# Exponentials as the stationary operand of the value product, 128-row output tiles over two batches, and a hand-written TensorE order

## The chip, the cores and the metric

The kernel runs on one core of one Trainium2 chip. The metric is the time of one execution on the device in microseconds (us), as the device reports it; medians of several executions are given. Every execution was classed as fast or slow (slow when over 1.5% above the fastest of its kernel). In the profiles PE is TensorE (the matrix engine), DVE is VectorE, ACT is ScalarE and POOL is GpSimd. TensorE writes its results to PSUM tiles; that DVE or ACT copies a tile out, so that it can be used again, is called its eviction.

## The reference, cut to what matters

```python
# attention: q, k, v are (8 batches, 12 heads, 448 rows, 64), fp32
q_n = q / (np.linalg.norm(q, axis=-1, keepdims=True) + 1e-06)
k_n = k / (np.linalg.norm(k, axis=-1, keepdims=True) + 1e-06)
attn = softmax(q_n @ k_n.T / tau)                # per head, 448 x 448, tau = 0.1
x = concat_heads(attn @ v)                       # (8, 448, 768)
# token mixing (T = 256), then channel mixing (C = 1536)
h  = np.maximum(x.T @ w_tok1, 0.0) @ w_tok2
u  = x + h.T
h2 = np.maximum(u @ w_ch1, 0.0) @ w_ch2
out = u + h2                                     # (8, 448, 768) fp32
```

## The kernel before

Rows are handled in four chunks of 112. Heads are handled in pairs, six pairs per batch, 48 pairs in all; a half of a batch is three pairs and is loaded together. The mixer of one batch is spread over the slots of the next batch's pairs. The parts that the change and the argument touch:

```python
SC, NCH, NPAIR = 112, 4, 6

def emit_attention_prep(b, pj, qkv_tiles):       # one pair: normalise q and k
    # ... cut: qt, kt are the pair's part of the loaded half
    sq16 = att.tile([SC, 2, 2, NCH, E], FP16, ...)
    nc.gpsimd.tensor_mul(out=sq16[:, 0], in0=qt[:], in1=qt[:])
    nc.gpsimd.tensor_mul(out=sq16[:, 1], in0=kt[:], in1=kt[:])
    nc.vector.tensor_reduce(out=ssq[:], in_=sq16[:], axis=AXX.X, op=ALU.add)
    nc.scalar.activation(out=lssq[:], in_=ssq[:], func=AF.Ln)
    nc.scalar.activation(out=rnorm[:], in_=lssq[:], func=AF.Exp, scale=-0.5)
    # ... cut: four tensor_tensor on gpsimd give qn and kn

def emit_attention_pv(b, pj):                    # v stationary, exp(scores) moving
    for hh in range(2):
        psO = ps.tile([E2, S], FP32, ...)        # 66 x 448, transposed output
        for i, c in enumerate(reversed(range(NCH))):
            nc.tensor.matmul(psO[:], vt[:, hh, c, :], pt16[:, c // 2, hh, c % 2, :],
                             start=(i == 0), stop=(i == NCH - 1))
        # ... cut: copied to SBUF as fp32 (ot), ACT for hh == 0, DVE for hh == 1

def emit_attention_bridge(b, pj, x16):           # transposed back, divided by the sum
    for hh in range(2):
        for c in range(NCH):
            nc.tensor.transpose(psT[:, c, :], ot[:, c * SC:(c + 1) * SC], id32[:E2, :E2])
        nc.vector.reciprocal(out=rec[:], in_=psT[:, :, E])
        nc.vector.tensor_tensor(out=x16[...], in0=psT[:, :, 0:E], in1=_bcast_free(rec[:], E),
                                op=ALU.mult)

# mixer slice 5: second channel product, 112-row tiles of one batch
for c in range(NCH):
    for dh in range(NDH):
        for ct_i in range(CT):                   # 12 matmuls
            nc.tensor.matmul(psF[:], gt16[:, ct_i, c * SC:(c + 1) * SC], wc2t[...], ...)
        for tt_i in range(TT):                   # 2 more: the token product, recomputed
            nc.tensor.matmul(psF[:], w2t[:, tt_i, c * SC:(c + 1) * SC], rt16[...], ...)
        nc.vector.tensor_tensor(out=ostage[...], in0=psF[:], in1=x16[...], op=ALU.add)

# main loop: everything is left to the scheduler; weights are loaded as fp32 and cast on DVE
for sl in range(NSLOT):
    # ... cut: load, prep(sl), tpose(sl-2), score(sl-3), pv(sl-4), bridge(sl-5), a mixer slice
```

Of the kernel before, what the change touches and what calls it, by code (L numbers as in the profile page):

```python
# [11 lines left out]
AXX = mybir.AxisListType  # L13

# [9 lines left out]
def kernel(  # L24
# [26 lines left out]
    E2 = E + 2  # L51
    inv_tau = 1.0 / float(tau)
    EPS_NORM = 1e-6

    cst = ctx.enter_context(tc.tile_pool(name="cst", bufs=1))
    wpool = ctx.enter_context(tc.tile_pool(name="wpool", bufs=1))
    stage = ctx.enter_context(tc.tile_pool(name="stage", bufs=3))
    qkv = ctx.enter_context(tc.tile_pool(name="qkv", bufs=3))
    att = ctx.enter_context(tc.tile_pool(name="att", bufs=4))
    ath = ctx.enter_context(tc.tile_pool(name="ath", bufs=4))  # L60
    ptp = ctx.enter_context(tc.tile_pool(name="ptp", bufs=4))
    xp = ctx.enter_context(tc.tile_pool(name="xp", bufs=2))
    mix = ctx.enter_context(tc.tile_pool(name="mix", bufs=1))
# [3 lines left out]
    psm = ps  # L67
# [9 lines left out]
    id32 = cst.tile([128, 128], FP32, name="id32")  # L77
    nc.gpsimd.memset(id32[:], 0.0)
    nc.gpsimd.affine_select(out=id32[:], in_=id32[:], compare_op=ALU.not_equal,
                            fill=1.0, base=0, pattern=[[-1, 128]], channel_multiplier=1)  # L80

    w1t = wpool.tile([SC, NCH, T], FP16, name="w1t")
    w2t = wpool.tile([128, TT, S], FP16, name="w2t")
    wc1t = wpool.tile([128, DT, C], FP16, name="wc1t")
    wc2t = wpool.tile([128, CT, D], FP16, name="wc2t")

    _weight_jobs = []

    def _staged_weight(dst_tile_ap, dram_ap, shape, nm, nchunks):
        def job():  # L90
            st = stage.tile(list(shape), FP32, name=f"ws_{nm}", tag="wst")
            nc.sync.dma_start(out=st[:], in_=dram_ap)
            last = shape[-1]
            cw = (last + nchunks - 1) // nchunks
            for ci in range(nchunks):
                lo, hi = ci * cw, min(last, (ci + 1) * cw)
                nc.vector.tensor_copy(out=dst_tile_ap[..., lo:hi], in_=st[..., lo:hi])  # L97
        return job

    _weight_jobs.append(_staged_weight(w1t[:], moe_w_tok1.rearrange("(c p) t -> p c t", p=SC),  # L100
                                       (SC, NCH, T), "w1", 1))
    _weight_jobs.append(_staged_weight(w2t[:], moe_w_tok2.rearrange("(tt p) s -> p tt s", p=128),
                                       (128, TT, S), "w2", 1))
    for dt_i in range(DT):
        _weight_jobs.append(_staged_weight(wc1t[:, dt_i, :], moe_w_ch1[dt_i * 128:(dt_i + 1) * 128, :],
                                           (128, C), f"wc1_{dt_i}", 3))
    for ct_i in range(CT):
        _weight_jobs.append(_staged_weight(wc2t[:, ct_i, :], moe_w_ch2[ct_i * 128:(ct_i + 1) * 128, :],
                                           (128, D), f"wc2_{ct_i}", 2))

    def emit_weight_loads():
        while _weight_jobs:
            _weight_jobs.pop(0)()

    def emit_qkv_half(b, half):
        h0 = 6 * half
        tiles = {}
        for nm, src in (("q", q), ("k", k)):
            t = qkv.tile([SC, 6, NCH, E], FP32, name=f"{nm}h_{b}_{half}", tag=f"{nm}h")
            nc.sync.dma_start(out=t[:].rearrange("p g c e -> p (g c) e"),  # L120
                              in_=src[b, h0:h0 + 6].rearrange("g (c p) e -> p (g c) e", p=SC))
            tiles[nm] = t
        vt = qkv.tile([SC, 6, NCH, E2], FP16, name=f"vh_{b}_{half}", tag="vh")
        nc.gpsimd.dma_start(out=vt[:, :, :, 0:E].rearrange("p g c e -> p (g c) e"),
                            in_=v[b, h0:h0 + 6].rearrange("g (c p) e -> p (g c) e", p=SC))
        nc.gpsimd.memset(vt[:, :, :, E:E + 2].rearrange("p g c e -> p (g c) e"), 0.0)
        nc.gpsimd.memset(vt[:, :, :, E:E + 1].rearrange("p g c e -> p (g c) e"), 1.0)
        tiles["v"] = vt
        return tiles

    pipe = {}

    def emit_attention_prep(b, pj, qkv_tiles):
        poff = 2 * (pj % 3)
        qt = qkv_tiles["q"][:, poff:poff + 2]
        kt = qkv_tiles["k"][:, poff:poff + 2]
        vt = qkv_tiles["v"][:, poff:poff + 2]

        sq16 = att.tile([SC, 2, 2, NCH, E], FP16, name=f"sq16_{b}_{pj}", tag="sq16")
        nc.gpsimd.tensor_mul(out=sq16[:, 0], in0=qt[:], in1=qt[:])  # L140
        nc.gpsimd.tensor_mul(out=sq16[:, 1], in0=kt[:], in1=kt[:])  # L141
        ssq = att.tile([SC, 2, 2, NCH], FP32, name=f"ssq_{b}_{pj}", tag="ssq")
        nc.vector.tensor_reduce(out=ssq[:], in_=sq16[:], axis=AXX.X, op=ALU.add)  # L143
        lssq = att.tile([SC, 2, 2, NCH], FP32, name=f"lssq_{b}_{pj}", tag="lssq")
        nc.scalar.activation(out=lssq[:], in_=ssq[:], func=AF.Ln)  # L145
        rnorm = att.tile([SC, 2, 2, NCH], FP32, name=f"rnorm_{b}_{pj}", tag="rnorm")
        nc.scalar.activation(out=rnorm[:], in_=lssq[:], func=AF.Exp, scale=-0.5)  # L147

        qn = att.tile([SC, NCH, 2, E], FP16, name=f"qn_{b}_{pj}", tag="qn")
        kn = att.tile([SC, NCH, 2, E], FP16, name=f"kn_{b}_{pj}", tag="kn")  # L150
        for g in range(2):
            nc.gpsimd.tensor_tensor(out=qn[:, :, g, :], in0=qt[:, g],  # L152
                                    in1=_bcast_free(rnorm[:, 0, g], E), op=ALU.mult)
            nc.gpsimd.tensor_tensor(out=kn[:, :, g, :], in0=kt[:, g],  # L154
                                    in1=_bcast_free(rnorm[:, 1, g], E), op=ALU.mult)
        pipe[(b, pj)] = {"qn": qn, "kn": kn, "vt": vt, "h0": 2 * pj}

    def emit_attention_tpose(b, pj):
        st = pipe[(b, pj)]
        qT = att.tile([128, S], FP16, name=f"qT_{b}_{pj}", tag="qT")  # L160
        kT = att.tile([128, S], FP16, name=f"kT_{b}_{pj}", tag="kT")
        for src, dst, tg in ((st["qn"], qT, "q"), (st["kn"], kT, "k")):
            pst = ps.tile([128, NCH, SC], FP16, name=f"pst{tg}_{b}_{pj}", tag="b")
            for c in range(NCH):
                nc.tensor.transpose(pst[:, c, :], src[:, c], id16[:SC, :SC])  # L165
            nc.vector.tensor_copy(out=dst[:], in_=pst[:])
        st["qT"], st["kT"] = qT, kT

    def emit_attention_score(b, pj):
        st = pipe[(b, pj)]  # L170
        qT, kT, h0 = st["qT"], st["kT"], st["h0"]
        pt16 = ptp.tile([SC, 2, 2, 2, S], FP16, name=f"pt16_{b}_{pj}", tag="pt16")
        for cg in range(2):
            psS = ps2.tile([SC, 2, 2, 512], FP32, name=f"psS_{b}_{pj}_{cg}", tag="b2")
            for j in range(2):
                c = 2 * cg + j
                for hh in range(2):
                    hb = hh * 64
                    nc.tensor.matmul(psS[:, hh, j, 0:S],  # L179
                                     kT[hb:hb + 64, c * SC:(c + 1) * SC],  # L180
                                     qT[hb:hb + 64, :],
                                     start=True, stop=True)
            nc.scalar.activation(out=pt16[:, cg], in_=psS[:, :, :, 0:S],  # L183
                                 func=AF.Exp, scale=inv_tau)
        st["pt16"] = pt16

    def emit_attention_pv(b, pj):
        st = pipe[(b, pj)]
        pt16, vt, h0 = st["pt16"], st["vt"], st["h0"]
        st["ot"] = {}  # L190
        for hh in range(2):
            hid = h0 + hh
            psO = ps.tile([E2, S], FP32, name=f"psO_{b}_{hid}", tag="b")
            for i, c in enumerate(reversed(range(NCH))):
                nc.tensor.matmul(psO[:], vt[:, hh, c, :], pt16[:, c // 2, hh, c % 2, :],
                                 start=(i == 0), stop=(i == NCH - 1))
            ot = ath.tile([E2, S], FP32, name=f"ot_{b}_{hid}", tag="ot")
            if hh == 0:
                nc.scalar.copy(out=ot[:], in_=psO[:])
            else:  # L200
                nc.vector.tensor_copy(out=ot[:], in_=psO[:])
            st["ot"][hh] = ot

    def emit_attention_bridge(b, pj, x16):
        st = pipe.pop((b, pj))
        h0 = st["h0"]
        for hh in range(2):
# [145 lines left out]
```

## Time and profile before

| | before |
|---|---|
| median of 3 runs | 622.88 us (619.04 to 623.16) |
| span of the profiled execution | 622.3 us |
| PE (TensorE matmul) busy | 523.1 us, 84% |
| DVE / ACT / POOL busy | 265.2 / 245.5 / 246.2 us |
| first TensorE matmul | 21.9 us |
| warm TensorE work, from the timeline | 466 us |

The last row is an estimate: for each kind of matmul the median distance from one start to the next, times the count (for the scores, which start in fours, about 0.5 us for four). It is what TensorE would need if it were never idle and always at full clock.

From the page of the kernel before: the busy line, two rows of the span in 40 slices (busy tenths of PE, granted TensorE clock in tenths) and the chain of work that ended last.

```profile
PE 523.1 (84%) x3424; PEld 330.4 (53%) x3424; DVE 265.2 (43%) x572; ACT 245.5 (39%) x337; POOL 246.2 (40%) x344
...
PE   0365888998878988789778897888989999999997
...
PEclk9978899799898988989988899888998999999999
...
PE 63%; POOL 19%; ACT 8%; DVE 3%; issue 3%; DMA 2%; SPq 0%; POOLq 0%; DVEq 0%; ACTq 0%
```

No engine but PE is near its limit, and PE itself has an 8 or a 7 in most slices. The timeline of the kernel before shows the pattern. Columns: start, duration, engine, line, operation, what is written and read; in brackets the idle time before it and what ended it.

```profile
300.54 1.65 ACT L183 ACTIVATE pt_4_1_3049<-psS_1_0_3050 112x1792 f16<-112x1792 f32 x1
...
302.24 0.58 PE L179 MATMUL psS_1_1_3056<-qT_1_2819,kT_1_2820 64*112 64x448 f16 x4 [1.81 <-ACT pt_4_1_3049 L183]
...
309.24 1.65 ACT L183 ACTIVATE pt_4_2_3148<-psS_2_0_3149 112x1792 f16<-112x1792 f32 x1
...
310.93 0.59 PE L179 MATMUL psS_2_1_3155<-qT_2_3035,kT_2_3036 64*112 64x448 f16 x4 [1.80 <-ACT pt_4_2_3148 L183]
```

Once per pair the second score group waits 1.8 us for the exponential that frees the only score buffer. The waits view of TensorE lists 61.3 us of waits for ACT in 36 places.

### The profile page before, as it was taken

What the parts mean: (1) busy time and instruction counts of PE and PEld (TensorE: products, weight loads), DVE (VectorE), ACT (ScalarE), POOL (GpSimd) and SP (SyncE); (2) the same over time, 40 slices, a digit from 0 to 9 for tenths busy, and PEclk for the clock granted to TensorE, in tenths of its full rate; (3) what the DMA queues carried; (4) which work ended last, traced back from release to release, by engine and by line L of the source; (5) the groups of instructions that cost most, each with busy time, mean ns of one, the idle gap of its engine ahead of it and who ended that gap; (6) DMA issues with size and microseconds to landing.
All of it is one profiled execution on the core that took longest, in us unless ns stands there. A gap on an engine that the chain in (4) does not pass through costs nothing.

```text
span 622.3 us, 8520 instructions
## 1 busy us (share of the span) xinstructions
PE 523.1 (84%) x3424; PEld 330.4 (53%) x3424; DVE 265.2 (43%) x572; ACT 245.5 (39%) x337; POOL 246.2 (40%) x344
## 2 busy tenths in 40 slices
PE   0365888998878988789778897888989999999997
PEld 0123454475544745447444474544755576658665
DVE  0377597466541444414453244532245124613401
ACT  0246755523465024640345503455036622760120
POOL 4987899893453324523244232442024110000000
PEclk9978899799898988989988899888998999999999
DMA  9999959691614608046080361711313011001102
GB/s 186 263 241 170 160 161 220 111 156 45 98 16 75 102 25 111 2 71 103 27 109 3 69 96 38 103 10 12 56 45 23 0 35 56 1 1 45 45 21 69
DMA packets 137255, 49.44 MB, mean 79 GB/s; under 512 B 130624, under 2 KB 131328, under 8 KB 137216
## 3 DMA queue, kind: packets, MB, share of 16 engines
q1 hardware_dynamic: 93952, 43.39, 32.1%
q0 software_dynamic: 43264, 5.51, 14.8%
q8 instruction: 27, 0.44, 0.3%
q14 instruction: 12, 0.10, 0.1%
HBM read 43.38 MB, written 11.01 MB: 87 GB/s over the span
## 4 chain that ended last, share of the span: by engine, by line
PE 63%; POOL 19%; ACT 8%; DVE 3%; issue 3%; DMA 2%; SPq 0%; POOLq 0%; DVEq 0%; ACTq 0%
DMA kh_0_119<-in_k_dram 2%; DVE wc1t L97 1%; POOL kn_0_408 L154 1%; PE psF_0_0_4387 L268 1%; PE psF_0_0_3632 L268 1%; PE psF_0_0_2877 L268 1%; PE psF_0_0_2122 L268 0%; POOL kn_0_960 L154 0%; POOL qn_3_644 L152 0%; PE psG_1_4154 L257 0%; PE psG_1_3399 L257 0%; PE psG_6_2001 L257 0%; PE psG_7_1254 L257 0%; PE psG_6_1246 L257 0%; POOL sq_2_2_1174 L141 0%
## 5 line engine op out<-in xcount | busy, mean ns | idle before, releaser
L257 PEld LDWEIGHTS <-wc1t 128*128 128x128 f16 x576 | 59.2, 104 | 58.6 <-issue 14.5
L229 PEld LDWEIGHTS <-w1t 112*128 112x128 f16 x128 | 12.6, 101 | 13.2 <-issue 7.1
L165 PE MATMUL pstq_0_188<-id_92,qn_0_134 112*128 112x112 f16 x4 | 0.6, 294 | 21.9 <-POOL qn_0_134 L152 21.9
L272 PEld LDWEIGHTS <-w2t 128*112 128x112 f16 x128 | 16.7, 130 | 4.2
L268 PEld LDWEIGHTS <-gt_3_3118 128*112 128x112 f16 x96 | 13.4, 141 | 3.7
L268 PEld LDWEIGHTS <-gt_4_3873 128*112 128x112 f16 x96 | 13.3, 140 | 3.7
L268 PEld LDWEIGHTS <-gt_2_2363 128*112 128x112 f16 x96 | 13.3, 140 | 3.7
L268 PEld LDWEIGHTS <-gt_1_1608 128*112 128x112 f16 x96 | 13.0, 136 | 3.4
L268 PEld LDWEIGHTS <-gt_7_5957 128*112 128x112 f16 x96 | 12.5, 130 | 3.2
L268 PEld LDWEIGHTS <-gt_6_5375 128*112 128x112 f16 x96 | 12.4, 130 | 3.0
L268 PEld LDWEIGHTS <-gt_0_853 128*112 128x112 f16 x96 | 12.4, 130 | 3.0
L268 PEld LDWEIGHTS <-gt_5_4628 128*112 128x112 f16 x96 | 12.4, 130 | 3.0
L165 PEld LDWEIGHTS <-qn_0_134 112*128 112x128 f16 x4 | 0.3, 130 | 21.9 <-POOL qn_0_134 L152 21.9
L259 ACT ACTIVATE gt_7_5957<-psG_0_6006 128x448 f16<-128x448 f32 x1 | 0.5, 543 | 27.1 <-PE psG_0_6006 L257 27.1
L152 POOL TENSOR_TENSOR qn_0_4734<-qh_0_4522,rnorm_0_4732 112x256 f16<-112x256 f32 x2 | 1.2, 610 | 21.1 <-PE pstq_2_4547 L165 21.1
L183 ACT ACTIVATE pt_7_1_5306<-psS_1_0_5307 112x1792 f16<-112x1792 f32 x1 | 1.7, 1663 | 17.9 <-PE psS_1_0_5307 L179 17.9
L147 ACT ACTIVATE rnorm_4_5284<-lssq_4_5282 112x16 f32<-112x16 f32 x1 | 0.2, 215 | 21.3 <-POOL kn_0_4735 L154 21.3
L275 DVE TENSOR_TENSOR ostage_0_6102<-psF_0_0_6103,x_7_113 112x384 f32<-112x384 f32 x1 | 0.6, 557 | 15.3 <-PE psF_0_0_6103 L272 15.3
L145 ACT ACTIVATE lssq_0_130<-ssq_0_128 112x16 f32<-112x16 f32 x1 | 0.2, 215 | 14.4 <-DVE ssq_0_128 L143 14.4
L179 PE MATMUL psS_2_0_351<-qT_2_275,kT_2_276 64*112 64x448 f16 x4 | 1.0, 574 | 5.7 <-ACT pt_0_1_289 L183 5.7
L152 POOL TENSOR_TENSOR qn_5_3128<-qh_1_2556,rnorm_5_3126 112x256 f16<-112x256 f32 x2 | 1.2, 614 | 11.7 <-PE pstq_1_2821 L165 11.7
L152 POOL TENSOR_TENSOR qn_5_4638<-qh_1_4066,rnorm_5_4636 112x256 f16<-112x256 f32 x2 | 1.2, 612 | 11.7 <-PE pstq_1_4331 L165 11.7
(2130 smaller groups left out, 1571.1 us busy)
## 6 DMA issues: line engine op xcount, KB each, us to landing
ws_wc_0_166<-in_moe_w_ch_dram SPq DMA_DIRECT2D x1, 768.0 KB, 11.6
ws_wc_1_200<-in_moe_w_ch_dram SPq DMA_DIRECT2D x1, 768.0 KB, 9.1
ws_wc_2_247<-in_moe_w_ch_dram SPq DMA_DIRECT2D x1, 768.0 KB, 11.3
ws_wc_3_316<-in_moe_w_ch_dram SPq DMA_DIRECT2D x1, 768.0 KB, 4.1
ws_wc_4_393<-in_moe_w_ch_dram SPq DMA_DIRECT2D x1, 768.0 KB, 4.8
ws_wc_5_470<-in_moe_w_ch_dram SPq DMA_DIRECT2D x1, 768.0 KB, 6.5
qh_0_117<-in_q_dram SPq DMA_DIRECT2D x1, 672.0 KB, 7.1
kh_0_119<-in_k_dram SPq DMA_DIRECT2D x1, 672.0 KB, 12.3
```

The costliest lines, as they stand in the source:

```text
L97: nc.vector.tensor_copy(out=dst_tile_ap[..., lo:hi], in_=st[..., lo:hi])
L152: nc.gpsimd.tensor_tensor(out=qn[:, :, g, :], in0=qt[:, g], in1=_bcast_free(rnorm[:, 0, g], E), op=ALU.mult)
L154: nc.gpsimd.tensor_tensor(out=kn[:, :, g, :], in0=kt[:, g], in1=_bcast_free(rnorm[:, 1, g], E), op=ALU.mult)
L165: nc.tensor.transpose(pst[:, c, :], src[:, c], id16[:SC, :SC])
L179: nc.tensor.matmul(psS[:, hh, j, 0:S], kT[hb:hb + 64, c * SC:(c + 1) * SC], qT[hb:hb + 64, :], start=True, stop=True)
L183: nc.scalar.activation(out=pt16[:, cg], in_=psS[:, :, :, 0:S], func=AF.Exp, scale=inv_tau)
L229: nc.tensor.matmul(psR[:], w1t[:, c, tt_i * 128:(tt_i + 1) * 128], x16[:, c, dh * DH:(dh + 1) * DH], start=(c == 0), stop=(c == NCH - 1))
L257: nc.tensor.matmul(psG[:], wc1t[:, dt_i, ct_i * 128:(ct_i + 1) * 128], ut16[:, dt_i, :], start=(dt_i == 0), stop=(dt_i == DT - 1))
L259: nc.scalar.activation(out=gt16[:, ct_i, :], in_=psG[:], func=AF.Relu)
L268: nc.tensor.matmul(psF[:], gt16[:, ct_i, c * SC:(c + 1) * SC], wc2t[:, ct_i, dh * DH:(dh + 1) * DH], start=(ct_i == 0), stop=False)
L272: nc.tensor.matmul(psF[:], w2t[:, tt_i, c * SC:(c + 1) * SC], rt16[:, tt_i, dh * DH:(dh + 1) * DH], start=False, stop=(tt_i == TT - 1))
L275: nc.vector.tensor_tensor(out=ostage[:, dh * DH:(dh + 1) * DH], in0=psF[:], in1=x16[:, c, dh * DH:(dh + 1) * DH], op=ALU.add)
```

## The change

Its intent is to take work from TensorE and to keep it fed:

- exp(scores) becomes the stationary operand (128 columns of it at a time) and v the moving one, 65 columns. The output then comes out with rows on partitions; the copy and the fp32 transposes go.
- Output rows of two batches share 128-row tiles: 7 tiles for two batches in place of 8. The two token matmuls per tile are replaced by three identity products that add u.
- The order of TensorE and POOL is fixed to the order in the program, with mixer units woven between the attention steps.
- Weights are cast to fp16 by the DMA; v, which the DMA cast before, is now loaded as fp32 and cast on DVE (`cast_v`).
- Normalisation is done for a half (three pairs) at once: 15 reductions of 3,072 elements per partition, and two smaller ones at the start, stand in for 48 of 1,024.

```diff
-        sq16 = att.tile([SC, 2, 2, NCH, E], FP16, name=f"sq16_{b}_{pj}", tag="sq16")
+    def prep(n, lo, hi, sq_eng):                       # a half: three pairs
+        sq = nrm.tile([SC, 2, g * NCH, E], FP32, name=f"sq_{n}_{lo}", tag="sq", bufs=1)
+        for i, src in enumerate((qf, kf)):
+            if sq_eng == "act":
+                nc.scalar.activation(out=sq[:, i], in_=src, func=AF.Square)
+            else:
+                nc.gpsimd.tensor_mul(out=sq[:, i], in0=src, in1=src)
+        nc.vector.tensor_reduce(out=ssq[:], in_=sq[:].rearrange("p a g e -> p (a g) e"),
+                                axis=AXX.X, op=ALU.add)
 ... cut: Ln, Exp, two DVE steps give rn; three pairs of qn, kn on gpsimd
-                nc.tensor.matmul(psO[:], vt[:, hh, c, :], pt16[:, c // 2, hh, c % 2, :],
-                                 start=(i == 0), stop=(i == NCH - 1))
 ... cut: the copies, the transposes
+        for m, lo in enumerate(COLS):                  # COLS = (0, 128, 256, 320)
+            for c in range(NCH):
+                nc.tensor.matmul(psO[:, m, 0:E + 1], st["pt"][:, c // 2, hh, c % 2, lo:lo + 128],
+                                 vt[:, g, c, 0:E + 1], start=(c == 0), stop=(c == NCH - 1))
+        nc.vector.reciprocal(out=rec[:], in_=psO[:, :, E])
+        nc.vector.tensor_tensor(out=x16[b][...], in0=psO[:, :, 0:E], in1=_bcast_free(rec[:], E), ...)
 ... cut: token products, first channel product (as before)
+            nc.tensor.matmul(psF[:], rows(gt, ct), wc2t[:, ct, dh * DH:(dh + 1) * DH], ...)   # 128 rows
+        for i in range(3):
+            nc.tensor.matmul(psF[:, 128 * i:128 * (i + 1)], rows(ut, 3 * dh + i), id16[:], ...)
 ... cut
+    with tc.manual_schedule(engines={PE, mybir.EngineType.Pool}):
+        load_half(0, split=True)
+        prep(0, 0, 2, "act")
+        load_half(1)
+        prep(0, 2, 6, "act")
+        cast_v(0)
+        weights_tok()
+        prep(1, 0, 6, "pool")
+        cast_v(1)
+        weights_ch1()
+        tpose(0)
+        for i in range(NP_ALL + 1):
+            if i % HP == 1 and i // HP + 2 < NHALF:
+                load_half(i // HP + 2)
+            if i % HP == 2 and i // HP + 2 < NHALF:
+                prep(i // HP + 2, 0, 6, "pool")
+                cast_v(i // HP + 2)
+            if i == 2:
+                weights_ch2()
 ... cut: quota = the share of the queued mixer work for this slot
+                score(i, 0); left = feed(left + quota * 0.25)
+                if i: pv(i - 1, 0)
+                left = feed(left + quota * 0.25)
+                if i + 1 < NP_ALL: tpose(i + 1)
+                score(i, 1); left = feed(left + quota * 0.25)
+                if i: pv(i - 1, 1)
+                left = feed(left + quota * 0.25)
```

(The weave is set here on fewer lines than in the source.)

## The prediction

> **What bounds it now.** TensorE, badly fed. The page shows PE busy 523.1 of 622.3 us (84%), DVE, ACT and POOL near 40%. In the timeline, warm starts are 162.5 ns apart for 384 columns, 189 for 448, 49 for 112-column identity products, 57 for the fp32 transposes; four scores take about 0.5 us. Times the counts: second channel product (with its 2 token matmuls) 146 us, first channel product 109, value matmul 73, fp32 transposes 22, scores 48, first transposes 19, rest 49: 466 us. The other 156 us are idleness and slow clock: first matmul at 21.7 us; in steady state (windows view, 200 to 434 us) 78 us per batch for 58 of warm work, granted clock 0.92. The timeline shows why: the second score group waits about 1.9 us for the exp (1.66 us) that frees the only score buffer; then identity products start 94 ns apart instead of 49. The Trainium skill, "TensorE: Matmul & The Clock Gate", Part 1, says that an idle window halves this clock; the trace agrees.
>
> **TensorE work.**
> - Value product: 384 x 189 = 72.6 us plus 384 transposes, 22.3 us, become 1,536 pairs of 128-column weight load and 65-column matmul. The same page, "Weight-path perf modes", gives a fast load for exactly 128 non-fp32 columns; the trace agrees: 98 ns for such loads, 130 for 112 columns. A pair costs at least 30 ns (estimate: 65 columns at the measured rate and fixed part), at most the 49 ns of today's 112-column pairs. I take 36: 55 us. Saves 40 (20 to 49).
> - Second channel product: 64 tile halves x 14 x 162.5 ns = 146 us become 56 x (12 x 162.5 + 3 x 56) = 119 us. Saves 27.
> - The rest: unchanged within 2 us.
> So 466 becomes about 399 us (389 to 418).
>
> **Waits.** Mixer units of 0.6 to 2.1 us are woven between score groups: with mixer work in the queue, about 4 us of PE work stands between the two groups of a pair against 1.9. I expect most of the 156 us to go; clock near 1.0 after the start.
>
> **Other engines, per batch of about 53 us.** ACT about 29 us (12 exps, 12 Relus of 543 ns, copies), DVE about 30 (3,072-element reductions take over 3 us and can hold up evictions), POOL about 30. None binds on average.
>
> **Start.** The split first load and ACT squares bring the first matmul to about 14 us. Then the fixed PE order hurts: pair 3 needs the second half's normalisation (estimate: about 31 us), pair 6 the third, while 10.7 MB of weights share the DMA queues with q, k, v. I expect about 20 us of PE idleness here.
>
> **Sum.** 399 work + 14 first matmul + 20 start stalls + 21 steady stalls (5%) + 6 tail = 460 us. Range 428 to 500. Chances: faster 0.98, same 0.01, slower 0.01.
>
> **Right or wrong.** Right: PE first busy near 14 us; value-matmul starts 30 to 40 ns apart; granted clock at least 0.97 after 100 us; 50 to 55 us per batch. Wrong: value pairs at 50 ns or more (weight load or issue bound); large PE waits for ACT (exp behind Relus) or for DVE (behind reductions); q/k loads landing over 20 us after issue because of the weight casts.
>
> **What would upset it.** Small pairs limited by issue or instruction fetch (8,274 PE rows against 6,220); POOL's in-order queue stuck behind descriptor work for the casts; in-order PE stalls repeating at each half.

## The result, and the profile after

| | before | after |
|---|---|---|
| median, same rounds, 4 runs each | 623.02 us | 550.51 us (549.74 to 553.52) |
| ratio of after to before | | 0.889, 95% interval 0.8829 to 0.8951 |
| span of the profiled execution | 622.3 us | 547.6 us |
| PE busy | 523.1 us, 84% | 445.7 us, 81% |
| warm TensorE work | 466 us | 394 us |
| span less warm work | 156 us | 153.6 us |

A ratio is the mean time of one kernel's fast runs over that of the other's fast runs of the same rounds, so it is not quite the ratio of the medians quoted. All outputs are right. The change is 11% faster, but the predicted 460 us was missed by 90 us. The last two rows tell where: 67 us of work were to go and 72 went, and of the 156 us beside the work nearly all stayed.

The page of the changed kernel, in the same rows as before:

```profile
PE 445.7 (81%) x4136; PEld 267.8 (49%) x4136; DVE 225.7 (41%) x415; ACT 235.7 (43%) x259; POOL 186.7 (34%) x145
...
PE   1546884977997889697977969889795999999996
...
PEclk9999586989898979899896989989897999999999
...
PE 59%; POOL 16%; DVE 14%; issue 5%; ACT 4%; DMA 1%; POOLq 0%; ACTq 0%
```

DVE rose from 3% to 14% of the chain although it does less work. POOL stands there with its squares. The waits view of the changed kernel, first of DVE, then of TensorE. Columns: engine, tile, line, what was waited for; us in total, times, the longest.

```profile
DVE ssq_0_3572 L145 <- POOL sq_0_3569 L143: 7.1, 1, 7.1
...
DVE ssq_0_4737 L145 <- POOL sq_0_4734 L143: 6.6, 1, 6.6
...
DVE ssq_0_779 L145 <- POOL sq_0_776 L143: 5.9, 1, 5.9
```

```profile
PE psG_0_911 L249 <- DVE ut_0_766 L243: 8.2, 1, 8.2
PE psG_0_3243 L249 <- DVE ut_1_2291 L243: 6.7, 1, 6.7
PE psG_0_4726 L249 <- DVE ut_2_3774 L243: 6.7, 1, 6.7
...
PE psS_0_1269 L188 <- ACT pt_1198 L190: 1.1, 1, 1.1
```

Summed, DVE waits 62.2 us in 12 places for POOL's squares at the line of the reduction. TensorE waits 55.9 us in 15 places for DVE (4.9 before) and 12.0 us for the exponentials (61.3 before, for all of ACT). One wait was removed and another of nearly the same size took its place. The timeline of the changed kernel shows how, in one of these places:

```profile
79.83 0.62 DVE L175 COPY qk_860<-pst_851 128x896 f16<-128x896 f16 x1
...
80.81 0.62 DVE L243 CAST ut_0_766<-psU_4_868 128x448 f16<-128x448 f32 x1 [0.37 <-PE psU_4_868 L241]
80.90 1.05 POOL L159 TENSOR_TENSOR kn_4_538<-kh_449,rn_0_526 112x512 f16<-112x512 f32 x1
...
81.50 0.36 PE L241 MATMUL psU_5_896<-id_89,x_0_236 128*128 128x128 f16 x4
...
81.91 2.75 POOL L143 TENSOR_TENSOR sq_0_776<-qh_670 112x1536 f32<-112x1536 f32 x1
...
84.61 2.75 POOL L143 TENSOR_TENSOR sq_0_776<-kh_671 112x1536 f32<-112x1536 f32 x1
87.40 3.35 DVE L145 TENSOR_REDUCE ssq_0_779<-sq_0_776 112x48 f32<-112x3072 f32 x1 [5.87 <-POOL sq_0_776 L143]
...
91.00 0.62 DVE L243 CAST ut_0_766<-psU_5_896 128x448 f16<-128x448 f32 x1
...
91.67 0.53 PE L249 MATMUL psG_0_911<-ut_0_766,wc1t 128*128 128x448 f16 x1 [8.18 <-DVE ut_0_766 L243]
```

TensorE finishes psU_5 at 81.9 us, and DVE is free. But the next instruction in DVE's queue is the reduction, and its input is only being made: POOL had to finish kn_4 and then takes 5.5 us for the two squares. DVE stands still for 5.87 us, reduces for 3.35 us, and only then evicts psU_5, at 91.00 us. TensorE waits 8.18 us for that.

POOL is late for a reason of its own, which its waits view shows:

```profile
POOL qn_4_4349 L159 <- PE pst_4663 L173: 6.6, 1, 6.6
POOL qn_4_1401 L159 <- PE pst_1715 L173: 6.6, 1, 6.6
```

In its fixed order the squares stand behind qn_4 and kn_4 of the half before. In 11 of the 12 places, all but the one above, POOL stood still for 4.4 to 6.6 us at qn_4, until TensorE had transposed an earlier pair and so set its buffer free, and took up the squares at once after kn_4. So it is its order, more than its speed, that makes them late; an earlier place for the squares on POOL, or more buffers for qn and kn, was not tried.

The Trainium skill, "Perfetto Trace Analysis", section "Tensor Engine Instruction", states that ACT, DVE and GpSimd take their instructions strictly first in, first out; this trace agrees, with a ready eviction standing 9 us behind a reduction that was not ready.

This comes back once per half, about every 30 us: gaps of TensorE of 3.1 to 8.2 us end at 91, 112, 135, 167, 194, 227, 259, 291, 324, 357, 389 and 421 us. (The one that ends at 167 us is a wait for ACT: the next instruction in ACT's queue, the Ln, waited for the reduction, and the Relus that evict stood behind it.) After each, the clock is low for a while, 3.4 to 6 us by the trace's record of the granted clock: after the gap that ends at 91.7 us, the value pairs start 54 to 57 ns apart and the 448-column products 373 ns apart until 95.5 us, then 33 and 189 ns. That is the slow clock that "TensorE: Matmul & The Clock Gate", Part 1, describes: half speed after an idle window, for some 3.4 us of busy time. Here it lasted 3.9 us.

### The profile page after: what moved, and what is told of

Same layout as the page of the kernel before. It is cut to its first block, busy times and chain, and to the rows that moved or that the text cites. A ratio compares the mean times of both kernels' runs of the same rounds, so it can differ in the third digit from the quotient of the medians.

```text
span 547.6 us, 9482 instructions
## 1 busy us (share of the span) xinstructions
PE 445.7 (81%) x4136; PEld 267.8 (49%) x4136; DVE 225.7 (41%) x415; ACT 235.7 (43%) x259; POOL 186.7 (34%) x145
## 4 chain that ended last, share of the span: by engine, by line
PE 59%; POOL 16%; DVE 14%; issue 5%; ACT 4%; DMA 1%; POOLq 0%; ACTq 0%
DVE vt_102 L165 2%; POOL sq_0_4330 L143 1%; POOL sq_0_3996 L143 1%; POOL sq_0_2847 L143 1%; POOL sq_0_3569 L143 1%; POOL sq_0_3251 L143 1%; POOL sq_0_2513 L143 1%; POOL sq_0_1086 L143 1%; POOL sq_0_776 L143 1%; POOL sq_0_2104 L143 1%; POOL sq_0_1382 L143 1%; POOL sq_0_4734 L143 1%; POOL sq_0_1776 L143 1%; PE psF_0_1_2161 L268 1%; DVE vt_100 L165 1%
## 5 line engine op out<-in xcount | busy, mean ns | idle before, releaser
L249 PEld LDWEIGHTS <-wc1t 128*128 128x128 f16 x576 | 53.9, 102 | 71.8 <-issue 31.0
L268 PEld LDWEIGHTS <-gt_0_767 128*128 128x128 f16 x168 | 16.1, 101 | 16.7 <-issue 7.7
L268 PEld LDWEIGHTS <-gt_1_2292 128*128 128x128 f16 x168 | 15.9, 101 | 14.3 <-issue 4.9
L268 PEld LDWEIGHTS <-gt_2_3775 128*128 128x128 f16 x168 | 15.6, 99 | 13.4 <-issue 3.9
L268 PEld LDWEIGHTS <-gt_3_5228 128*128 128x128 f16 x168 | 15.9, 98 | 9.6
L217 PEld LDWEIGHTS <-w1t 128*128 128x128 f16 x128 | 11.6, 102 | 13.7 <-issue 8.5
L249 PE MATMUL psG_0_911<-ut_0_766,wc1t 128*128 128x448 f16 x6 | 1.6, 384 | 8.2 <-DVE ut_0_766 L243 8.2
L268 PE MATMUL psF_0_1_2161<-wc2t,gt_0_767 128*128 128x384 f16 x12 | 4.0, 520 | 4.6 <-DVE ost_0_2086 L274 4.6
L249 PE MATMUL psG_0_3243<-ut_1_2291,wc1t 128*128 128x448 f16 x6 | 1.6, 383 | 6.7 <-DVE ut_1_2291 L243 6.7
L249 PE MATMUL psG_0_4726<-ut_2_3774,wc1t 128*128 128x448 f16 x6 | 1.6, 382 | 6.7 <-DVE ut_2_3774 L243 6.7
L145 DVE TENSOR_REDUCE ssq_0_3572<-sq_0_3569 112x48 f32<-112x3072 f32 x1 | 3.4, 3352 | 7.1 <-POOL sq_0_3569 L143 7.1
L145 DVE TENSOR_REDUCE ssq_0_3254<-sq_0_3251 112x48 f32<-112x3072 f32 x1 | 3.4, 3353 | 6.6 <-POOL sq_0_3251 L143 6.6
L145 DVE TENSOR_REDUCE ssq_0_4737<-sq_0_4734 112x48 f32<-112x3072 f32 x1 | 3.4, 3352 | 6.6 <-POOL sq_0_4734 L143 6.6
L203 PEld LDWEIGHTS <-pt_800 112*128 112x128 f16 x32 | 1.7, 115 | 8.8 <-issue 8.7
L145 DVE TENSOR_REDUCE ssq_0_779<-sq_0_776 112x48 f32<-112x3072 f32 x1 | 3.4, 3354 | 5.9 <-POOL sq_0_776 L143 5.9
L249 PE MATMUL psG_0_4035<-ut_2_3774,wc1t 128*128 128x448 f16 x6 | 1.8, 382 | 4.6 <-DVE ut_2_3774 L243 4.6
L249 PE MATMUL psG_0_2552<-ut_1_2291,wc1t 128*128 128x448 f16 x6 | 1.8, 382 | 4.6 <-DVE ut_1_2291 L243 4.6
L145 DVE TENSOR_REDUCE ssq_0_1779<-sq_0_1776 112x48 f32<-112x3072 f32 x1 | 3.4, 3352 | 5.0 <-POOL sq_0_1776 L143 5.0
L145 DVE TENSOR_REDUCE ssq_0_1385<-sq_0_1382 112x48 f32<-112x3072 f32 x1 | 3.4, 3352 | 5.0 <-POOL sq_0_1382 L143 5.0
```

The source lines that it names most:

```text
L145: nc.vector.tensor_reduce(out=ssq[:], in_=sq[:].rearrange("p a g e -> p (a g) e"), axis=AXX.X, op=ALU.add)
L203: nc.tensor.matmul(psO[:, m, 0:E + 1], st["pt"][:, c // 2, hh, c % 2, lo:lo + 128], vt[:, g, c, 0:E + 1], start=(c == 0), stop=(c == NCH - 1))
L217: nc.tensor.matmul(psR[:], w1t[:, m, tt * 128:(tt + 1) * 128], x16[b][:, m, dh * DH:(dh + 1) * DH], start=(m == 0), stop=(m == 3))
L249: nc.tensor.matmul(psG[:], wc1t[:, dt, ct * 128:(ct + 1) * 128], ut[:, dt, span(b)], start=(dt == 0), stop=(dt == DT - 1))
L268: nc.tensor.matmul(psF[:], rows(gt, ct), wc2t[:, ct, dh * DH:(dh + 1) * DH], start=(ct == 0), stop=False)
```

## The experiments

Three theories stood at the start. **A**: DVE stands in order at a reduction whose squares are not there, ahead of ready evictions; the cost is where the reduction stands in DVE's queue. **B**: the hand-written TensorE order is too stiff, and a free order would fill the gaps. **C**: POOL is too slow with its squares, so that its speed and not DVE's order is what has to be mended. All runs below were timed in three rounds beside the kernel before, whose median was 620.29, 618.71 and 620.59 us in the three sets (e1 to e4, e5 to e8, e9 to e12).

### e1: DVE in program order, the reduction one slot later

```diff
-    with tc.manual_schedule(engines={PE, mybir.EngineType.Pool}):
+    with tc.manual_schedule(engines={PE, mybir.EngineType.Pool, mybir.EngineType.DVE}):
             if i % HP == 2 and i // HP + 2 < NHALF:
-                prep(i // HP + 2, 0, 6, "pool")
-                cast_v(i // HP + 2)
+                prep_sq(i // HP + 2, 0, 6, "pool")         # the squares alone
+            if i % HP == 0 and i and i // HP + 1 < NHALF:
+                prep_rest(i // HP + 1, 0, 6)               # the reduction, a slot later
 ... after score(i, 0) and pv(i - 1, 0):
+                if i % HP == 0 and i and i // HP + 1 < NHALF:
+                    prep_fin(i // HP + 1, 0, 6)            # rn, qn, kn
+                    cast_v(i // HP + 1)
```

> The changed kernel with one difference: DVE keeps the order written in the program, the norm's long reduction is written one pair slot after POOL's squares, and the two small steps that follow it half a slot later. Theory A (DVE's queue is blocked: a 3.35 us reduction stands in it ahead of finished PSUM tiles and waits 4 to 7 us for POOL's squares, so TensorE runs out of its 4 PSUM tiles): the DVE waits on the squares (62 us in 12 waits in the changed kernel) fall under 10 us, PE gaps of 3 to 8 us vanish after 110 us, the granted clock after 110 us rises from 0.93 to at least 0.97, and the time falls to 470 to 500 us. Theory B (the hand-made TensorE order itself starves the engine): no more than 2% gained, 540 us or more. Theory C (POOL is too slow for the squares wherever they stand): the reduction still waits, 530 us or more.

Measured: 483.25 us (483.16 to 484.26), ratio 0.778 [0.7739, 0.782]. The same instructions run; PE busy fell to 419.0 us and the mean granted clock rose from 0.924 to 0.979. The two small steps after the reduction and the cast of v move with it. The waits of DVE in the window from 70 to 450 us (in the whole run they are 13.9 us, 12.5 of them in one wait at the start), and the timeline at one of the reductions:

```profile
DVE ssq L158 <- POOL sq L150: 0.3, 1, 0.3
```

```profile
260.20 0.42 DVE L226 TENSOR_TENSOR x<-psO,rec 128x256 f16<-128x256 f32 x1
260.54 3.34 DVE L158 TENSOR_REDUCE ssq<-sq 112x48 f32<-112x3072 f32 x1
...
263.80 0.17 DVE L225 RECIPROCAL rec<-psO 128x4 f32<-128x4 f32 x1
```

The reduction takes the same 3.34 us, but without a wait ahead of it, and TensorE waits 0.81 us at the most in the stretch from 258 to 264 us. POOL is as slow as it was (193.5 us busy). That supports A; C, as far as it means POOL's speed, is not needed. The page shows where the rest of the time is:

```profile
PE   0017588897999899999999999999998999999995
```

TensorE stands nearly idle for the first 35 us: the program order puts the reduction of the second half ahead of the first copy of transposed q and k, and TensorE waits 22.9 us for that copy.

### e2: the TensorE order left to the scheduler

```diff
-    with tc.manual_schedule(engines={PE, mybir.EngineType.Pool}):
+    with tc.manual_schedule(engines={mybir.EngineType.Pool}):
```

> The changed kernel with TensorE's order left to the scheduler; POOL's order stays by hand. Theory A (DVE's queue is blocked by the early reduction): DVE's order is the same, so the stalls stay: within 2% of the changed kernel's 550 us. Theory B (the hand-made TensorE order starves the engine): 3% faster or more, under 534 us.

Measured: 545.48 us, ratio 0.8781 [0.874, 0.8821]. The waits of DVE in this run:

```profile
DVE ssq L145 <- POOL sq L143: 63.4, 12, 7.1
```

The same 12 waits, and nearly the same sum (62.2 us before). B falls: a free order gains about 1% (0.8781 against 0.889, from different sets of rounds).

### e3: the value product undone

v is stationary again and the output is transposed back, in the otherwise changed kernel.

```diff
+        for c in range(NCH):
+            nc.tensor.matmul(psV[:], vt[:, g, c, :], st["pt"][:, c // 2, hh, c % 2, :], ...)
+        # copied to fp32 (ot): ACT for hh == 0, DVE for hh == 1
-            for c in range(NCH):
-                nc.tensor.matmul(psO[:, m, 0:E + 1], st["pt"][:, c // 2, hh, c % 2, lo:lo + 128], ...)
+            nc.tensor.transpose(psO[:, m, :], ot[:, lo:lo + 128], id32[:E + 2, :E + 2])
```

> The changed kernel with the value product alone undone: v stationary, 448 moving columns, a copy to SBUF and four fp32 transposes per head into the new 128-row places. By warm spacings this adds 384 x 189 + 384 x 58 - 1536 x 33 ns = 44 us of TensorE work, and a 0.6 us copy per head on ACT or DVE. If TensorE's work counts in full: 590 to 600 us. Theory A (every half is paced by the chain POOL, DVE reduction, TensorE, with TensorE idle beside it) lets part of it hide in the stalls: 565 to 585 us.

Measured: 627.57 us, ratio 1.0086 [1.0037, 1.0136]: 77 us slower than the changed kernel and even a little slower than the kernel before. Both expected ranges were missed. By the timeline the old form costs 44 us more of warm work (384 products at 189 ns and 384 transposes at 58 ns are 94.9 us, against 1,536 pairs at 33 ns, 50.7 us). The rest goes with new waits for the copy between product and transposes. The waits of TensorE in this run, and then the only wait for that copy that the kernel before shows:

```profile
PE psO L222 <- DVE ot L212: 35.0, 22, 6.2
PE psO L222 <- ACT ot L210: 22.5, 16, 5.2
```

```profile
PE psT_2_1006 L212 <- ACT ot_4_997 L199: 0.9, 1, 0.9
```

The kernel before had the copy as well, but a whole slot stood between it and the transposes, and TensorE hardly waited. So the 57.5 us of waits belong to the tight order of e3, and its 77 us do not show what the value product is worth against the kernel before. What the run shows is that in this order, and while the DVE waits stood, the other parts, which also took 27 us of work from TensorE, came to nothing in sum.

### e4: the squares on ACT

```diff
-                prep(i // HP + 2, 0, 6, "pool")
+                prep(i // HP + 2, 0, 6, "act")
```

(and the same for half 1.)

> The changed kernel with all squares on ACT (Square, about 1.5 us for 1536 elements) in place of POOL (2.75 us). Theory A: the reduction's place in DVE's queue is again picked by the scheduler; its wait for squares gets shorter or longer with ACT's queue, but its own 3.35 us stay; ACT gets 48 us more work. Time 520 to 550 us. Theory C (POOL's speed is the whole cause): under 510 us, the DVE waits for squares under 10 us.

Measured: 492.72 us, ratio 0.7926 [0.7892, 0.796]. By its number this was the outcome expected of C, not of A; but C also expected waits for squares under 10 us. The waits of DVE:

```profile
DVE ssq L145 <- ACT sq L141: 27.9, 11, 8.3
```

The scheduler still chooses the place of the reduction of 3.35 us; in the built program it even stands two to three pairs earlier than in the changed kernel, from the third half on. But its squares are ready earlier, since ACT does not have to do qn and kn first. The number expected of A was wrong in that I took the reduction itself as a cost; most of it is absorbed. Together with e1, which left POOL as it was, the run shows that the cost lies in the wait between the two, and that it can be taken away from either end. From the first value product of the third batch (its pair is number 12) to the end, e4 takes 363.9 us, e1 365.5 and the changed kernel 426.8; what e4 is slower than e1, it loses at the start.

### e8: normalisation per pair

```diff
-            if i % HP == 2 and i // HP + 2 < NHALF:
-                prep(i // HP + 2, 0, 6, "pool")
+            if i >= 2 and (i - 2) // HP + 2 < NHALF:
+                lo = 2 * ((i - 2) % HP)
+                prep((i - 2) // HP + 2, lo, lo + 2, "pool")
```

> The changed kernel (DVE's order left to the scheduler) with the normalisation made for one pair at a time as in the kernel before, in three slots: squares of 512 elements, a 1,024-element reduction of about 1.1 us in place of 3,072 elements and 3.35 us. Theory A says that a stall comes when the reduction's wait plus its own length exceeds the roughly 4 us that 4 PSUM tiles cover: smaller pieces (wait about 2 us plus 1.1) stay under that, time 475 to 510 us, DVE waits for squares under 25 us in total. If the scheduler's early placing hurts at any size: 530 us or more.

Measured: 522.17 us (517.51 to 522.89), ratio 0.8426 [0.8355, 0.8496]. It lies between the two expectations; the waits expected of A, under 25 us in total, were missed. The waits of DVE:

```profile
DVE ssq L145 <- POOL sq L143: 117.6, 40, 4.2
```

Nearly twice the waiting in total, and yet 28 us faster. None of the 40 waits is longer than 4.2 us, and a reduction takes 1.22 us in place of 3.35: the waits of TensorE for DVE, all together, come to 20 us in place of 55.9. (Those for the exponentials rose, to 24.1 us from 12.0.) The Trainium skill, "Perfetto Trace Analysis", section "Optimizing Scalar/DVE Operations", says that breaking up instructions may help where they cause bubbles on other engines. This run agrees (28 us), but the place in the queue was worth more (67 us in e1).

### e10: DVE in program order, nothing moved

This is e1's first line alone.

> The changed kernel with DVE held in program order as TensorE and POOL are, with nothing moved in the program: the reduction is written right after the squares it needs, ahead of the evictions of that slot. Theory A (the cost is the in-order wait of DVE for POOL's squares, wherever the reduction stands ahead of ready evictions): no gain, 540 to 570 us, DVE waits of 4 us or more per half stay. If it was the scheduler's order as such that cost the time (not the reduction's place): 480 to 500 us as in the split variant.

Measured: 561.99 us, ratio 0.9079 [0.9027, 0.9132]. The waits of DVE:

```profile
DVE ssq L145 <- POOL sq L143: 63.5, 15, 12.5
```

The program order as such gains nothing in sum (it loses 2%); the waits stay. The loss is at the start, where TensorE waits 24.2 us for the first copy of q and k, as in e1: the value product of pair 12 starts at 142.1 us, against 120.8 in the changed kernel. From there to the end e10 takes 417.9 us against 426.8, so the order alone gave 9 of the 61 us that e1 gained in that stretch (365.5). With e1 this shows that it is mainly the later place of the reduction that took the waits away. (The opposite half, the reduction written later and DVE left to the scheduler, was built but not run: in its instruction order the scheduler puts 15 of the 17 reductions in the same place as before, and the other two earlier.)

### e5 and e9: the start

e5 takes e1 and mends its start: the first transposes are written first, the reduction of half 1 goes a slot later, and the channel weights are loaded at pairs 2 and 5.

```diff
         prep(0, 0, 2, "act")
+        tpose(0)
         load_half(1)
 ...
-        prep(1, 0, 6, "pool")
-        cast_v(1)
-        weights_ch1()
-        tpose(0)
+        prep_sq(1, 0, 6, "pool")
 ... in the loop: prep_rest(1), prep_fin(1) at i == 1, weights_ch1 at i == 2, weights_ch2 at i == 5
```

> The first experiment's kernel, whose TensorE stood idle for 23.2 us after the first transposes because its DVE order put the second half's reduction ahead of the copy that the first scores need. Here the first transposes and their copy are written ahead of that, and the second half's reduction one slot later. If DVE's order is the cause of that gap too, it shrinks to under 6 us and the time falls by 12 to 20 us to 463 to 471 us. If the gap is loads that have not landed, it comes back at the fourth pair: 478 us or more.

Measured: 478.27 us, ratio 0.7731 [0.7675, 0.7787]; 5 us less than e1, not the 12 to 20 us hoped for. By its number this was the outcome expected of loads that have not landed; but POOL began the squares of half 1 at 23.03 us straight after its own DMA issues, without a wait for the load. The gap of 23 us came back as gaps of 4.5, 9.0 and 7.8 us: each of the next halves is waited for in turn, while POOL takes about 17 us per half (5.5 of squares, 5 of waiting, 6.2 of qn and kn). e9 moves the squares of halves 1 and 2 to ACT:

```diff
-        prep_sq(1, 0, 6, "pool")
+        prep_sq(1, 0, 6, "act")
-                prep_sq(i // HP + 2, 0, 6, "pool")
+                prep_sq(i // HP + 2, 0, 6, "act" if i == 2 else "pool")
```

> The start-fixed variant with the squares of halves 1 and 2 moved from POOL to ACT, nothing else. If the gaps of 5, 9 and 8 us that came back at the start are set by POOL's chain (squares 5.5 us, wait, qn and kn per half), each of halves 1 and 2 gets ready about 5 us earlier: 466 us (462 to 472), against 478 for the start-fixed variant. If the start is paced by loads or by the weight casts instead, or if the squares on ACT merely hold up its exps: 475 us or more.

Measured: 473.94 us, ratio 0.7653 [0.7616, 0.7691]. It lies between the two expectations, and its interval overlaps that of e5. The waits of TensorE for the copy of q and k in the first 70 us, in e5 and then in e9:

```profile
PE psS L207 <- DVE qk L194: 19.3, 4, 9.0
```

```profile
PE psS L207 <- DVE qk L194: 12.6, 4, 6.2
```

The waits got shorter by 7 us, so POOL's squares were probably part of the start's cost; 12.6 us of waits for that copy remain, and so does a wait of 9.5 us for the first normalised q. What paces these to the end was not settled.

### e6 and e7: the two parts of the TensorE work, once DVE is out of the way

e6 is e1 with the value product undone as in e3 (the small steps after the reduction come a little later in their slot). e7 is e1 with 112-row output tiles of one batch (the identity products stay):

```diff
     def place(b, m):
-        return 128 * m if b % 2 == 0 else (64 + 128 * m if m < 3 else 0)
+        return 128 * m
         def rows(t, i):
-            lo = (b % 2) * S + place(b, m) if m < 3 else 384
-            return t[:, i, lo:lo + 128]
+            lo = (b % 2) * S + SC * m
+            return t[:, i, lo:lo + SC]
 ... for m in range(4) in both batches
```

> The first experiment's kernel (TensorE fed 99% after the start) with the value product undone: v stationary, a copy and four fp32 transposes per head. Warm spacings give 384 x 189 + 384 x 60 - 1536 x 33 ns = 45 us more TensorE work. If TensorE's work is what the time now consists of: 483 + 45 = 528 us, 520 to 540. If the new value product's gain lies in fewer waits (no copy in the middle) rather than in work: over 545 us. With the stalls in place the same undoing cost 77 us.

> The first experiment's kernel with output rows in 112-row tiles, four for each batch (64 tile halves in place of 56). Warm spacings give 8 x (12 x 163 + 3 x 56 ns) = 17 us more work: 483 + 17 = 500 us, 496 to 505. If the 112-column weights load too slowly to hide behind 384 columns, more: over 507 us.

Measured: e6 558.45 us, ratio 0.9029 [0.8963, 0.9094], which is 75 us over e1. Some 44 us of that are the extra work; the rest are again waits of TensorE for the copies (29 us in 33 places in its waits view, against 0.9 us in the kernel before). The expected 528 us counted the work alone and missed. (The 99% that the expectation quotes is too high: from 110 us on, TensorE was busy for 96% of the time in e1.) e7 gave 499.58 us, ratio 0.8079 [0.8009, 0.8148]: 16.3 us over e1 where 17 were expected. The shared row tiles are worth their work once TensorE is fed.

### e11: the TensorE order left free, once DVE is out of the way

```diff
-    with tc.manual_schedule(engines={PE, mybir.EngineType.Pool, mybir.EngineType.DVE}):
+    with tc.manual_schedule(engines={mybir.EngineType.Pool, mybir.EngineType.DVE}):
```

(against e1.)

> The split variant (reduction a slot later, DVE in program order), with the order of TensorE left to the scheduler. If the hand-woven order is worth nothing, as in the changed kernel: 478 to 490 us. If its worth was only masked by the DVE waits: over 495 us, with waits of TensorE for the exp back in the steady state.

Measured: 473.24 us (472.9 to 473.44), ratio 0.7639 [0.7604, 0.7674]. It is a little better than the range expected for "worth nothing", and 10 us faster than e1. From its page, the busy and clock rows:

```profile
PE   0007888998999999999999999999999999999995
...
PEclk9999997999999999999999999999999999999999
```

Most of the 10 us are the start: between 50 and 110 us TensorE is busy for 54.1 us at a clock of 0.94, against 48.9 us at 0.86 in e1, and the value product of pair 12 starts 7.0 us sooner. From there to the end e11 takes 362.7 us against 365.5, so in the steady state the two orders differ by 3 us. This is the fastest version run, 24% under the kernel before and 14% under the changed kernel.

### e12: channel weights cast on DVE

The changed kernel, with the channel weights loaded as fp32 and cast on DVE as before.

```diff
-            nc.gpsimd.dma_start(out=wc1t[:, 3 * i:3 * i + 3, :], in_=moe_w_ch1[...])
+            st = stage.tile(list(shape), FP32, name=f"ws_{nm}", tag="wst", bufs=2)
+            nc.sync.dma_start(out=st[:], in_=dram)
+            nc.vector.tensor_copy(out=dst[...], in_=st[...])      # in two parts
```

> The changed kernel with the channel weights loaded as fp32 by the sync queue and cast on DVE as in the kernel before (tokens' weights as changed). If the cast by DMA only moves work out of a DVE that is not short on average: within 2% of the changed kernel, 542 to 562 us, the start a few us longer. If it matters for the start: over 562 us.

Measured: 558.77 us, ratio 0.9023 [0.898, 0.9066], within the 2% expected: DVE has 26.9 us more to do (252.6 against 225.7), and 8 us of it show in the time.

## Why the prediction was right or wrong

The prediction's sum was "399 work + 14 first matmul + 20 start stalls + 21 steady stalls (5%) + 6 tail = 460". The table splits four spans in the same way. Idle is the span less PE busy, split at 110 us by the windows view. "Slow" is PE busy less the warm work. It holds the half-clock stretches and, as ends of matmuls are modelled, overlap of busy records. By the mean granted clock (0.940, 0.924, 0.979, 0.992) the throttle cost at most 37, 42, 10 and 4 us of the four spans; the rest of the row is not slow clock.

| us | predicted | before | after | e1 | e11 |
|---|---|---|---|---|---|
| warm work | 399 | 466 | 394 | 394 | 394 |
| idle in the first 110 us | 34 (14 + 20) | 45 | 45 | 48 | 41 |
| idle later | 27 (21 + 6, slow clock included) | 54 | 57 | 14 | 8 |
| slow | in the line above | 57 | 52 | 25 | 29 |
| span | 460 | 622 | 548 | 481 | 472 |

- **The work was right** (399 us predicted, 394 from the spacings). Value pairs start 33 ns apart (predicted 36, range 30 to 49) and take 50.7 us (55). The fast weight load for 128 columns of a type that is not fp32, which the skill's page "TensorE: Matmul & The Clock Gate" states in "Weight-path perf modes", carried over: a pair with a 128-column load costs 33 ns. The second channel product takes 672 x 163 ns + 168 x 56 ns = 119 us, as predicted, and e7 confirmed its row part on the clock (16.3 us for 17).
- **The wait that I had seen was removed.** Waits of TensorE for the exponentials fell from about 61 us to 12 us. The woven mixer units do what was said of them; e2 and e11 show that the scheduler's own order does it as well, from the same woven program text, so the fixing of TensorE's order by hand deserves none of the credit.
- **The step that failed is the term "21 steady stalls (5%)", with "I expect most of the 156 us to go; clock near 1.0 after the start".** Stalls after the start and the row "slow" came to 57 + 52 = 109 us in place of 27, the granted clock after 110 us was 0.94 and not 0.97 or more, and a batch took about 65 us in the steady state, not 50 to 55 (e1: about 52). About 56 us (45 of them after 110 us) are waits for DVE, which stood in order at the reduction while POOL was still at the squares; each such gap of 3.1 to 8.2 us was followed by 3.4 to 6 us at half clock. The prediction named reductions that "can hold up evictions", and large waits of TensorE "for DVE (behind reductions)" as a sign that it would be wrong, but its sum has no term for a wait of DVE. It did not ask when their input would be there, nor where the scheduler, which still orders DVE, would set them. That the wait was the cause is shown: e1 moved the reduction later with the same work on every engine and took 67 us off; e10 kept it in place and lost 11 us (21 at the start, less 9 gained later); e4 made its squares ready sooner and took 58 us off.
- **The start was about right in size, for a partly other reason.** The first matmul came at 9.4 us, not 14; the idleness of the first 110 us was 45 us for 34. In e1, e5, e9 and e11 what remains of it are mostly waits for normalised q and k of the early halves and for their copies.
- **With the failed step mended, the sum nearly holds.** The span of e11, 471.6 us, is 12 us over the predicted 460: 7 us more in the start and about 10 us more in later stalls and the row "slow", less 5 us of work. That the sums come so near is partly luck, since the prediction had no entry for the overlap in that row.
- **The worth of the value product.** I took it as 40 us, its work; by the spacings it is 44. Undoing it in e3 and e6 cost 77 and 75 us, since there TensorE also waits for the copy (57.5 and 29.4 us). As that wait was 0.9 us in the kernel before, a worth beyond the work is not shown.

## What to carry to other kernels

When work is batched into fewer and longer instructions on a side engine, ask of each when its input will be ready and what stands behind it in that engine's queue: in these runs 3.35 us of reduction alone were absorbed (e1, e4), and the same 3.35 us behind 4 to 7 us of waiting were not. Ask the same of the engine that makes the input: what stands ahead of it in that queue, and what does that wait for? If one engine's order is fixed by hand, look at the order that the scheduler gives the engines that feed and drain it, for there a ready eviction can stand behind an unready reduction. A repeating gap on TensorE cost more here than its length, because 3.4 to 6 us at half clock followed each.

## What the Trainium skill lacked or had wrong

- "TensorE: Matmul & The Clock Gate", "Back-to-back issue gap": it gives about 81 ns as the measured sustained spacing of load and matmul pairs at 128 columns, and says that the formula of N / 2.4 + 2.5 ns counts too little there. In these traces warm pairs lie at the formula or a little above it: 56 ns at 128 columns (formula 55.8), 49 ns at 112 (49.2), 33 ns at 65 (29.6), each with its own weight load.
- The same page, "HAM oscillation": its rule is that there be no idle gaps of over about 3.4 us. In the kernel before, the longest distance between two matmul starts from 200 to 434 us was 2.03 us, yet the granted clock was 0.91 to 0.92; gaps of 1.8 us once per pair were enough. In that stretch the trace has 18 gaps of 1.5 to 1.8 us, and 12 of them are followed, 0.7 to 2.0 us after their end, by 3.4 us at half clock. The page's next section tells of a kernel with short idling between groups, but gives no length.
- "Perfetto Trace Analysis", "Optimization Strategy": it says that repeating bubbles can mean too few buffers, and names no other cause. Here the bubble once per half was an in-order engine waiting for an instruction that was not ready. A wait for a buffer stood in its chain too (POOL at qn_4, 4.4 to 6.6 us), but the order of one engine took the bubble away with the same buffers (e1, 550.51 to 483.25 us). The page states the strict order of DVE elsewhere but does not join the two.
- "VectorE: DVE Perf Modes", "The perf-mode tier table": it lists the reduction in its plain mode for every type, and gives no time. The runs agree: 1,024 elements per partition took 1.22 us in fp32 (the changed kernel's first reduction) and 1.21 us in fp16 (the kernel before), and 3,072 in fp32 took 3.35 us, 1.09 ns an element.
